# Banded attention values: two row quarters in one product of 64 rows and 48 columns

## The chip, the cores and the metric

The kernel runs on one core of a Trainium2 chip. The metric is device microseconds from start to end of one execution. Engines are named as the profile names them: PE is TensorE's matrix product, PEld its weight load, DVE is VectorE, ACT is ScalarE, POOL is GpSimd, SP is SyncE, which issues the DMAs here.

## What is computed

An attention of two scales, over 4 batches, 8 heads, 576 positions and head size 64, is followed by two gated feed-forward layers over its 2304 tokens. Only the attention's banded half is touched here; cut to it, the reference is:

```python
pos = np.arange(S)                                    # S = 576
mask = np.abs(pos[:, None] - pos[None, :]) < 4
scores = np.where(mask, q @ k.T / 8, -1e9)            # per batch and head
attn = np.exp(scores - scores.max(-1))
attn = attn / (attn.sum(-1) + 1e-9)
out_local = attn @ v                                  # the banded values
return out_up + out_local                             # out_up: attention over means of 4 positions
```

## The kernel before

**Jobs.** A job is one batch and one pair of heads, 16 in all, called (b, hp) below. A query meets only the keys at most 3 positions away, so the 576 queries are cut into 24 tiles of 24 queries (`NQ`), each with its 30 keys (`NU`). Four tiles stand at a time in the four quarters of 32 partitions; `NG` = 6 such groups and the two heads h make the 24 x 2 tiles of a job.

**Steps of a job.** PE makes the band scores (line 813) and the pooled scores (line 866) in one PSUM buffer `pa` of two banks. DVE subtracts the maxima (849, 850), ACT takes the exponential into `pt` (853), DVE sums, inverts and multiplies by the inverse (854, 856, 857) and transposes each block of 32 x 32 (858) from `pt` into `tt`, so that keys lie on partitions. Then `band` (960 to 969) multiplies: for group g, quarter i and head h one product has the 30 value rows of that quarter as weights (64 columns, `vt`) and the quarter's 24 probability columns as the moving side. Half of the quarters (0 and 2, then 1 and 3) go in one call, 24 products a call, two calls a job. In all jobs but (0,0) and (1,0), which the code marks as not `merged`, the first call stands in front of the transposes of the pooled probabilities (`down_t`, 951) and the second in front of the pooled values (`values`, 989). ACT copies the transposes out (957); `combine` on DVE adds both halves (1002).

**What sets the order.** The code first records every operation with engine, planned duration, due time and buffers; `Plan.order` then simulates the engines with those planned durations and writes a fixed order for each of the five queues. `ATT` is the time that the plan sets aside for a batch's attention in a feed-forward visit. So a job's small products stand between the large products of a feed-forward visit: the attention of batches 1 to 3 is spread over the feed-forward work of batches 0 to 2, from about 44 to 365 us. PE also waits for the weights of the large products: each block of 128 x 512 weights is split by ACT (`whi`, line 1055) and by DVE or POOL (`wlo`, its low part, 1058), in a ring of four buffers, and is used by twelve products (1119 to 1121). On PE every float32 product of the band is recorded as two pieces, so 24 products appear as x48.

Of the kernel before, what the change touches and what calls it, by code (L numbers as in the profile page):

```python
# [10 lines left out]
F32 = mybir.dt.float32  # L11
# [5 lines left out]
AF = mybir.ActivationFunctionType  # L17
# [350 lines left out]
def tile_multiscale_attention_gated_ffn(  # L368
# [95 lines left out]
    for nm, n, shape in (("qt", 2, [P, S + 8]), ("kt", 2, [P, KPAD + S + 5]), ("vt", 0, [P, NG, VC]),  # L464
                         ("sc", 1, [P, 2, NG, NU]), ("pt", 2, [P, 2, NG, 32]), ("tt", 2, [P, 2, NG, 32]),
                         ("vg", 1, [GH, 2, 4, VC]), ("half", 1, [P, G, 2]),
                         ("qd", 2, [P, G]), ("kd", 2, [P, G]), ("vd", 2, [GH, 2, VC]),
                         ("pd", 2, [GH, 2, 2, G]), ("pdt", 1, [GH, 2, 2, G]), ("up", 2, [P, G]), ("ones", 1, [P, 102]),
                         ("xf", 2, [P, S])):
        aslots += ring(nm, n, shape, F32, apool)  # L470

# [159 lines left out]
    QUANTUM = 3 * 227.0  # L631
    ATT = 15.0e3
    T0 = 30.0e3
# [106 lines left out]
    class Job:  # L740
# [48 lines left out]
        def pools(self):  # L789
            for nm in ("qd", "kd", "sc", "nm", "sm", "pd", "nmd", "smd", "pt", "tt"):  # L790
                setattr(self, nm, self.buf(nm))
# [5 lines left out]
        def scores(self):  # L797

            ss = bank(self.banks)
            qt, kt, sc, pt, tt, nm, sm = self.qt, self.kt, self.sc, self.pt, self.tt, self.nm, self.sm  # L800
            n = NG * NU
# [32 lines left out]
            if not masked:  # L834
                op("dve", dve_ns(2 * n), lambda: nc.vector.tensor_add(
                    sc.t.rearrange("p h g c -> p h (g c)"), ss.t[:, :, :n],
                    maskb[:, None, :].to_broadcast([P, 2, n])), [ss], [sc], when)
            if self.merged:
# [7 lines left out]
            def scores_of():  # L846
                return ss.t[:, :, :n].rearrange("p h (g c) -> p h g c", c=NU) if masked else sc.t

            op("dve", dve_ns(2 * n), lambda: nc.vector.reduce_max(nm.t, scores_of(), axis=AX.X), [x], [nm], at)
            op("dve", dve_ns(2 * n), lambda: nc.vector.tensor_sub(sc.t, scores_of(), spread(nm)),  # L850
               [nm, x] if masked else [nm], [sc], at, port=not masked)
            p = pt.t[:, :, :, :NU]
            op("act", act_ns(2 * n), lambda: nc.scalar.activation(p, sc.t, AF.Exp, scale=SCALE), [sc], [pt], at)
            op("dve", dve_ns(2 * n), lambda: nc.vector.reduce_sum(sm.t, pt.t[:, :, :, :NU + 1], axis=AX.X),
# [4 lines left out]
                out=tt.t.rearrange("p h g c -> p (h g c)"), in_=pt.t.rearrange("p h g c -> p (h g c)")),  # L859
               [pt], [tt], at)  # L860

        def pooled(self, ss, c):
# [73 lines left out]
        def down_t(self):  # L936
# [23 lines left out]
        def band(self, x, ss):  # L960

            vt, tt, v0 = halves[self.b, self.hp // 2].vt, self.tt, self.hp % 2 * P
            for g in range(NG):
                for s, i in ((0, x), (1, 2 + x)):
                    ks, q = slice(32 * i, 32 * i + NU), NQ * (NG * x + g)
                    for h in range(2):
                        nc.tensor.matmul(ss.t[h * D:(h + 1) * D, s, q:q + NQ],  # L967
                                         vt.t[ks, g, v0 + h * D:v0 + (h + 1) * D], tt.t[ks, h, g, :NQ],
                                         start=True, stop=True, tile_position=(32 * i, h * D))

        def values(self):

            b, hp = self.b, self.hp
            early = self.merged
            ss = self.ss if early else bank(self.banks)
            half = halves[b, hp // 2]
            vd, vt, pdt, tt = half.vd, half.vt, self.pdt, self.tt
            up = buf("up")  # L980
# [4 lines left out]
            def pe():  # L985
                self.band(int(early), ss)
                for kh in range(2):
# [10 lines left out]
            if not early:  # L998
                op("pe", 700.0, lambda: self.band(1, ss), [vt, tt, up], [ss], at, heat=90.0, words=96)
# [568 lines left out]


    op("act", act_ns(P), lambda: nc.scalar.copy(identb.t, ident.t), [ident], [identb], 0.0)  # L1570
    jobs = [Job(b, hp) for b in range(B) for hp in range(NHP)]
# [7 lines left out]
    for n in range(len(jobs) + 1):  # L1579
# [80 lines left out]
```

## Time and profile before

| what | us |
|---|---|
| time, median of 3 runs | 911.86 (911.67 to 912.22) |
| the profiled execution's own time | 911.72 |
| its span, first to last instruction | 909.7 |
| PE busy | 899.0 (99%) |
| DVE busy | 700.4 (77%) |
| ACT busy | 530.5 (58%) |
| POOL busy | 70.1 (8%) |

The span is the part of the execution that the instructions cover; 2.0 us lie around it. PE's records overlap, because matmuls are pipelined: the time that a stretch costs on PE is read from start to start in the timeline, not from the durations. The granted clock is 0.999 of full speed over the span.

### The profile page before, as it was taken

The page shows a single profiled execution, that of the slowest core. Times are in us where ns is not written, and L with a number is a line of the kernel's source. Part 1 is how long each engine was busy: PE and PEld are TensorE (multiplying, and loading weights), DVE is VectorE, ACT ScalarE, POOL GpSimd, SP SyncE. Part 2 cuts the span into 40 slices and gives each one's busy share as a digit, 9 for nine tenths or more (in the row PEclk, how much of TensorE's full clock was granted, in tenths as well). Part 3 has the DMA queues.
Part 4 walks back from the last instruction along what each step waited for, and adds up shares of the span by engine and source line. Part 5 has one row for each costly group of instructions (what it writes and reads, how often), then busy time and mean ns, then how long its engine had stood idle before and what let it go on. Part 6 is the DMA issues. An engine that isn't in the chain of part 4 may idle for free.

```text
span 909.7 us, 18862 instructions
## 1 busy us (share of the span) xinstructions
PE 899.0 (99%) x7369; PEld 758.6 (83%) x7369; DVE 700.4 (77%) x1322; ACT 530.5 (58%) x1119; POOL 70.1 (8%) x103
## 2 busy tenths in 40 slices
PE   7999999999999999999999999999999999999998
PEld 5787878878888877899999998888888988888886
DVE  8987885676567666899999898778976779877642
ACT  4687874666656666755554655444665655535541
POOL 4011110111011100010000000000301001000000
PEclk9999999999999999999999999999999999999999
DMA  8769581664466635343212651103531002000531
GB/s 254 235 207 257 177 206 48 197 164 167 156 189 197 210 110 183 97 156 117 96 41 65 218 182 46 47 24 106 175 117 66 1 1 70 36 36 35 174 93 47
DMA packets 65675, 113.75 MB, mean 125 GB/s; under 512 B 8433, under 2 KB 29755, under 8 KB 65586
## 3 DMA queue, kind: packets, MB, share of 16 engines
q1 hardware_dynamic: 65586, 112.54, 40.0%
q8 instruction: 58, 0.95, 0.5%
q14 instruction: 31, 0.25, 0.1%
HBM read 82.37 MB, written 30.15 MB: 124 GB/s over the span
## 4 chain that ended last, share of the span: by engine, by line
PE 98%; DVE 1%; POOL 0%; issue 0%; ACT 0%; POOLq 0%
PE ph L1119 14%; PE ph L1120 13%; PE ph L1121 13%; PE acc L1119 9%; PE acc L1121 9%; PE acc L1120 9%; PE pa L1119 7%; PE pa L1120 7%; PE pa L1121 7%; PE pa L967 2%; PE pa L813 1%; PE pa L866 1%; PE pa L989 1%; PE pa L951 1%; PE acc L1611 1%; PE acc L724 1%
## 5 line engine op out<-in xcount | busy, mean ns | idle before, releaser
L1119 PE MATMUL ph<-xhi,whi 128*128 128x512 f32 (+1 forms) x344 | 134.6, 391 | 0.0
L1120 PE MATMUL ph<-xhi,wlo 128*128 128x512 f32 (+1 forms) x344 | 131.6, 382 | 0.0
L1121 PE MATMUL ph<-xlo,whi 128*128 128x512 f32 (+1 forms) x344 | 131.5, 382 | 0.0
L1055 ACT CAST whi<-w 128x512 fp32r<-128x512 f32 x140 | 85.4, 611 | 57.5 <-PE ph L1121 30.0
L1058 DVE TENSOR_TENSOR wlo<-w,whi 128x512 fp32r<-128x512 f32 x137 | 94.3, 690 | 27.7 <-ACT whi L1055 27.3
L1058 DVE TENSOR_TENSOR wlo<-wr,whi 128x512 fp32r<-128x512 f32 x106 | 68.5, 648 | 36.8 <-ACT whi L1055 35.2
L1119 PEld LDWEIGHTS ph<-xhi,whi 128*128 128x128 f32 x344 | 64.7, 188 | 15.4 <-issue 2.0
L1121 PEld LDWEIGHTS ph<-xlo,whi 128*128 128x128 f32 x344 | 64.7, 188 | 12.9
L1055 ACT CAST whi<-wr 128x512 fp32r<-128x512 f32 x106 | 60.2, 570 | 26.1 <-PE acc L1121 12.9
L1120 PEld LDWEIGHTS ph<-xhi,wlo 128*128 128x128 f32 x344 | 64.7, 188 | 11.7
L1119 PE MATMUL acc<-ghi,whi 128*128 128x512 f32 (+1 forms) x192 | 73.5, 383 | 0.0
L1121 PE MATMUL acc<-glo,whi 128*128 128x512 f32 (+1 forms) x192 | 72.3, 376 | 0.4 <-DVE glo L1058 0.4
L1120 PE MATMUL acc<-ghi,wlo 128*128 128x512 f32 (+1 forms) x192 | 72.2, 376 | 0.0
L1235 DVE TENSOR_TENSOR w<-pa,w 128x512 f32<-128x512 f32 (+1 forms) x112 | 70.2, 627 | 2.6 <-PE pa L1121 2.1
L1055 ACT CAST w<-w 128x512 fp32r<-128x512 f32 x62 | 37.9, 619 | 43.2 <-PE acc L1120 22.0
L1119 PE MATMUL pa<-w,whi 128*128 128x512 f32 (+1 forms) x166 | 60.7, 366 | 0.1
L1121 PE MATMUL pa<-w,whi 128*128 128x512 f32 (+1 forms) x166 | 60.7, 365 | 0.0
L1120 PE MATMUL pa<-w,wlo 128*128 128x512 f32 (+1 forms) x166 | 60.6, 365 | 0.0
L1058 DVE TENSOR_TENSOR w<-w,w 128x512 fp32r<-128x512 f32 x58 | 41.2, 715 | 18.8 <-ACT w L1055 18.8
L1160 DVE SCALAR_TENSOR_TENSOR th<-th,ph 128x512 f32<-128x512 f32 (+1 forms) x44 | 28.0, 637 | 27.6 <-PE ph L1121 23.0
L1155 ACT ACTIVATE th<-ph 128x512 f32<-128x512 f32 (+1 forms) x44 | 24.6, 559 | 39.6 <-PE ph L1121 39.4
L1119 PEld LDWEIGHTS acc<-ghi,whi 128*128 128x128 f32 x192 | 36.0, 188 | 7.4 <-issue 1.7
(311 smaller groups left out, 2204.4 us busy)
## 6 DMA issues: line engine op xcount, KB each, us to landing
w<-w SPq DMA_DIRECT2D x56, 512.0 KB
w2d<-we SPq DMA_DIRECT2D x32, 256.0 KB
w<-gd SPq DMA_DIRECT2D x32, 256.0 KB
gd<-w SPq DMA_DIRECT2D x30, 256.0 KB
st<-x2d SPq DMA_DIRECT2D x52, 128.0 KB
w<-w SPq DMA_DIRECT2D x24, 256.0 KB
w<-w2d SPq DMA_DIRECT2D x16, 256.0 KB
wr<-w2d SPq DMA_DIRECT2D x16, 256.0 KB
```

The costliest lines, as they stand in the source:

```text
L724: nc.tensor.matmul(ss.t[:GH, kh, :VC], ones.t[ks, o:o + GH], vt.t[ks, g], start=g == 0, stop=g == NG - 1, tile_position=(64 * kh, 0))
L813: nc.tensor.matmul(ss.t[32 * i:32 * i + 32, h, g * NU:(g + 1) * NU], qt.t[hs, NQ * t:NQ * t + 32], kt.t[hs, NQ * t:NQ * t + NU], start=not ...
L866: nc.tensor.matmul(ss.t[:GH, h, c + r * G:c + (r + 1) * G], qd.t[h * D:(h + 1) * D, r * GH:(r + 1) * GH], kd.t[h * D:(h + 1) * D, :], star ...
L967: nc.tensor.matmul(ss.t[h * D:(h + 1) * D, s, q:q + NQ], vt.t[ks, g, v0 + h * D:v0 + (h + 1) * D], tt.t[ks, h, g, :NQ], start=True, stop=T ...
L1055: op("act", act_ns(n), lambda: nc.scalar.copy(vh(), vm()), [rm], [rh], due)
L1058: return lambda: on.tensor_sub(vl(), vm(), vh().bitcast(F32))
L1119: nc.tensor.matmul(o, lhi, rhi, start=first, stop=False, skip_group_check=more)
L1120: nc.tensor.matmul(o, llo, rhi, start=False, stop=False, skip_group_check=more)
L1121: nc.tensor.matmul(o, lhi, rlo, start=False, stop=last, skip_group_check=more)
L1155: op("act", act_ns(n, True), lambda h=h: nc.scalar.activation(th.t[:, :n], h.t[:, :n], AF.Tanh, scale=0.5 if layer == 1 else 1.702 / 4.0), ...
L1160: op("dve", dve_ns(n), lambda: nc.vector.scalar_tensor_tensor(th.t[:, :n], th.t[:, :n], 1.0, hb[-1].t[:, :n], op0=ALU.add, op1=ALU.mult), ...
L1235: op("dve", dve_ns(N), lambda: nc.vector.tensor_add(tmp.t[:, o, :N], b.t[:, :N], tmp.t[:, i, :N]), [b, (tmp, i)], [(tmp, o)], t)
```

## The change

For batches 1 to 3 the two calls of `band` become one call of `bands`, which takes two neighbouring quarters (64 rows) in one product: the probabilities of the two quarters stand as a block diagonal, s = 0 and s = 1, so that 64 value rows meet 2 x 24 = 48 columns, and the zeros in the block keep the quarters apart. A job has 24 products of 64 rows x 48 columns in place of 48 products of 30 rows x 24 columns. The call stands in `values`; `down_t` keeps only its transposes. Batch 0 stays as it was.

The block diagonal is made by DVE. `parity` holds 1 or 0 by quarter and s; the inverse sums are multiplied by it into 24 columns (`smw`), and one product of 720 elements writes the exponentials times `smw` to `ptw`, so that a quarter's other half becomes zero. The exponential now stays in `sc`, which has one more column for the 1e-9. The transpose is over 768 elements. `ptw` and `ttw` lie over the two former buffers of `pt` and `tt`, so there is one of each, not two.

The diff, cut to its core:

```diff
-                         ("sc", 1, [P, 2, NG, NU]), ("pt", 2, [P, 2, NG, 32]), ("tt", 2, [P, 2, NG, 32]),
+                         ("sc", 1, [P, 2, NG, NU + 1]), ("pt", 0, [P, 2, NG, 32]), ("tt", 0, [P, 2, NG, 32]),
...
+            both = apool.tile([P, 2, *shape[1:]], F32, name=nm, tag=nm)
+            plan.ring(nm, [Slot(both[:, i]) for i in range(2)])
+            plan.ring(nm + "w", [Slot(both.rearrange("p n h g c -> p (n h g c)").rearrange(
+                "p (h g s c) -> p h g s c", h=2, g=NG, s=2), tuple(plan.rings[nm][0]))])
...
+    nc.vector.memset(plan.rings["sc"][0][0].t[:, :, :, NU:NU + 1], 1.0e-9)
...
-    ATT = 15.0e3
+    ATT = 13.0e3
...
+        def wide(self, at, n):
...
+            op("act", act_ns(n), lambda: nc.scalar.activation(p, p, AF.Exp, scale=SCALE), [], [sc], at)
+            op("dve", dve_ns(n), lambda: nc.vector.reduce_sum(sm.t, sc.t[:, :, :, :NU + 1], axis=AX.X),
+               [sc], [sm], at)
+            op("dve", 155.0, lambda: nc.vector.reciprocal(sm.t, sm.t), [], [sm], at)
+            op("dve", 155.0, lambda: nc.vector.tensor_mul(
+                smw.t, sm.t.rearrange("p h g -> p (h g)")[:, :, None].to_broadcast([P, 2 * NG, 2]),
+                parity.t[:, None, :].to_broadcast([P, 2 * NG, 2])), [sm, parity], [smw], at, port=True)
+            op("dve", dve_ns(2 * n), lambda: nc.vector.tensor_mul(
+                ptw.t.rearrange("p h g s c -> p (h g) s c")[:, :, :, :NU],
+                hg(sc.t)[:, :, None, :NU].to_broadcast([P, 2 * NG, 2, NU]),
+                smw.t[:, :, :, None].to_broadcast([P, 2 * NG, 2, NU])), [sc, smw], [ptw], at, port=True)
+            op("dve", dve_ns(NG * 128), lambda: nc.vector.transpose(
+                out=ttw.t.rearrange("p h g s c -> p (h g s c)"), in_=ptw.t.rearrange("p h g s c -> p (h g s c)")),
+               [ptw], [ttw], at)
...
             if self.merged:
-                c, due, more = HALF // 2, 0.5, [halves[self.b, self.hp // 2].vt, self.tt]
+                due = 0.5
+            if self.merged and not self.b:
+                c, more = HALF // 2, [halves[self.b, self.hp // 2].vt, self.tt]
...
-                if self.merged:
+                if more:
                     self.band(0, ss)
...
+        def bands(self, ss):
+            vt, ttw, v0 = halves[self.b, self.hp // 2].vt, self.ttw, self.hp % 2 * P
+            for g in range(NG):
+                for i in range(2):
+                    ks, q = slice(64 * i, 64 * i + 64), NQ * g
+                    for h in range(2):
+                        o = ss.t[h * D:(h + 1) * D, i, :HALF].rearrange("p (s q) -> p s q", s=2)
+                        nc.tensor.matmul(o[:, :, q:q + NQ], vt.t[ks, g, v0 + h * D:v0 + (h + 1) * D],
+                                         ttw.t[ks, h, g, :, :NQ], start=True, stop=True, tile_position=(64 * i, h * D))
...
-                self.band(int(early), ss)
+                if wide:
+                    self.bands(ss)
+                else:
+                    self.band(int(early), ss)
...
-            op("pe", 1400.0, pe, [vd, pdt, vt, tt], [ss, up, xf], at, heat=300.0, words=112)
+            op("pe", 1500.0 if wide else 1400.0, pe, [vd, pdt, vt, tt], [ss, up, xf], at, heat=300.0, words=112)
...
-            if x < len(front):
-                front[x]()
-            if x < len(back):
-                back[x]()
+            for some in (front, back) if n <= NHP else (back, front):
+                if x < len(some):
+                    some[x]()
```

The written order moves too. In the two pieces below the large products of a feed-forward visit are 1119 to 1121 before and 1176 to 1178 now; 967 was `band` and 1021 is `bands`; 951 and 993 are the pooled transposes, 989 and 1046 the pooled values.

PE's queue at the last job, (3,3), before:

```order
L1121 MATMUL ph_149<-xlo_91,whi_81 128x512
L967 MATMUL pa_159<-tt_129,vt 64x24 x24
L951 MATMUL pa_159<-ident,pd_139 72x72 x8
L1119 MATMUL ph_149<-xhi_89,whi_81 128x512
...
L1121 MATMUL ph_150<-xlo_91,whi_78 128x512
L967 MATMUL pa_159<-tt_129,vt 64x24 x24
L989 MATMUL pa_159<-pdt_140,vd_137 64x144 x4
```

and now:

```order
L1178 MATMUL ph_147<-xlo_91,whi_81 128x512
L993 MATMUL pa_157<-ident,pd_137 72x72 x8
L1176 MATMUL ph_147<-xhi_89,whi_81 128x512
...
L1178 MATMUL ph_148<-xlo_91,whi_78 128x512
L1021 MATMUL pa_157<-tt,vt 64x2x24 x24
L1046 MATMUL pa_157<-pdt_138,vd_135 64x144 x4
```

The first of the job's two band calls is gone from the queue; the one that is left has the second's place, twelve large products behind the transposes, as before.

DVE's queue at job (2,1), from the sum of the exponentials to the first low parts of weights behind the transpose, before:

```order
L854 TENSOR_REDUCE small<-pt_127 128x12
L856 RECIPROCAL small<-small 128x12
L1164 TENSOR_TENSOR glo_96<-th_98,ghi_94 128x512
L857 TENSOR_TENSOR pt_127<-pt_127,small 128x12x30
L858 STREAM_TRANSPOSE tt_129<-pt_127 128x384
L1058 TENSOR_TENSOR wlo_83<-w_112,whi_79 128x512
L1058 TENSOR_TENSOR wlo_84<-wr_108,whi_80 128x512
```

and now, where 1115 makes the low parts (1058 before) and 1221 is the former 1164:

```order
L888 TENSOR_REDUCE small<-sc_125 128x12
L1221 TENSOR_TENSOR glo_96<-th_98,ghi_94 128x512
L890 RECIPROCAL small<-small 128x12
L894 TENSOR_TENSOR pt<-sc_125,ones_141 128x24x30
...
L1115 TENSOR_TENSOR wlo_83<-w_112,whi_79 128x512
L898 STREAM_TRANSPOSE tt<-pt 128x768
L1115 TENSOR_TENSOR wlo_84<-wr_108,whi_80 128x512
```

The product and the transpose are twice as wide, and one low part now stands between them.

## Rows read from the trace of the kernel before

**Rows 1.** The page: busy us of each engine, share of the span, instructions.

```profile
PE 899.0 (99%) x7369; PEld 758.6 (83%) x7369; DVE 700.4 (77%) x1322; ACT 530.5 (58%) x1119; POOL 70.1 (8%) x103
```

**Rows 2.** Waits of PE, all: engine, line, releaser, us, times, longest us.

```profile
PE pa L807 <- ACT identb L1570: 4.9, 1, 4.9
...
PE acc L1121 <- DVE glo L1058: 0.4, 1, 0.4
```

**Rows 3.** Busy time by stretch: stretch, length, PE, PEld, DVE, ACT, POOL busy (count).

```profile
60.00:143.00 83.00, 83.00 (x1051) 66.64 (x1050) 65.30 (x112) 62.00 (x135) 8.71 (x12) 1.00 0.69 194
...
sum 303.00, PE 303.00 PEld 244.22 DVE 211.76 ACT 199.88 POOL 28.12; mean PE 101.00 PEld 81.41 DVE 70.59 ACT 66.63 POOL 9.37
```

**Rows 4.** PE's timeline at job (1,1): start us, us, engine, line, shapes, count.

```profile
84.42 0.39 PE L1121 MATMUL acc<-glo,whi 128*128 128x512 f32 x1
84.73 0.89 PE L967 MATMUL pa<-tt,vt 30*64 30x24 f32 x48
85.56 0.69 PE L951 MATMUL pa<-ident,pd 72*72 72x72 f32 x8
...
86.37 0.39 PE L1120 MATMUL acc<-ghi,wlo 128*128 128x512 f32 x1
```

**Rows 5.** PE's timeline at job (1,0), whose transposes stand without a band call.

```profile
63.03 0.39 PE L1119 MATMUL acc<-ghi,whi 128*128 128x512 f32 x1
...
63.48 0.39 PE L1121 MATMUL acc<-glo,whi 128*128 128x512 f32 x1
63.71 0.66 PE L951 MATMUL pa<-ident,pd 72*72 72x72 f32 x8
...
64.49 0.40 PE L1120 MATMUL ph<-xhi,wlo 128*128 128x512 f32 x1
```

**Rows 6.** PE's timeline around the second, separate band call of job (1,0).

```profile
77.25 0.39 PE L1121 MATMUL ph<-xlo,whi 128*128 128x512 f32 x1
...
78.73 0.40 PE L1120 MATMUL ph<-xhi,wlo 128*128 128x512 f32 x1
```

**Rows 7.** Lines 967, 813, 866: ns min/median/max, first and last start us.

```profile
L967 PEld LDWEIGHTS pa<-tt,vt x1248: 127/133/134, 28.5 to 363.0; 30*64 30x64 f32 x179
L967 PE MATMUL pa<-tt,vt x1248: 210/211/233, 28.5 to 363.0; 30*64 30x24 f32 x179
...
L813 PEld LDWEIGHTS pa<-kt,qt x1248: 102/106/154, 5.3 to 346.2; 64*32 64x32 f32 x179
L813 PE MATMUL pa<-kt,qt x1248: 184/191/258, 5.3 to 346.2; 64*32 64x30 f32 x179
...
L866 PE MATMUL pa<-kd,qd x112: 282/283/341, 12.4 to 346.7; 64*72 64x144 f32 x112
```

**Rows 8.** Timeline of products and weight loads near 76 us.

```profile
75.98 0.50 PE L1119 MATMUL ph<-xhi,whi 128*128 128x512 f32 x1
76.09 0.19 PEld L1120 LDWEIGHTS ph<-xhi,wlo 128*128 128x128 f32 x1
```

**Rows 9.** Groups on DVE by line and shape: count, busy us, mean ns, idle before.

```profile
L1002 DVE TENSOR_TENSOR xf<-pa,up 128x576 f32<-128x576 f32 x13 | 9.8, 755 | 4.6 <-ACT up L996 3.3 <-PE pa L967 1.3
L858 DVE STREAM_TRANSPOSE tt<-pt 128x384 f32<-128x384 f32 x14 | 8.0, 575 | 0.3
L857 DVE TENSOR_TENSOR pt<-pt,small 128x360 f32<-128x360 f32 x14 | 7.6, 543 | 0.2
```

**Rows 10.** Timeline: band values of job (1,0), transpose of job (1,1).

```profile
74.52 0.89 PE L967 MATMUL pa<-tt,vt 30*64 30x24 f32 x48
...
75.09 0.58 DVE L858 STREAM_TRANSPOSE tt<-pt 128x384 f32<-128x384 f32 x1
```

**Rows 11.** Timeline: low parts behind job (2,1)'s transpose, and the products that follow.

```profile
199.24 1.45 DVE L1058 TENSOR_TENSOR wlo<-wr,whi 128x512 fp32r<-128x512 f32 x2
...
201.24 0.39 PE L1119 MATMUL acc<-ghi,whi 128*128 128x512 f32 x1
```

**Rows 12.** Busy time behind the attention, columns as in rows 3.

```profile
380.00:460.00 80.00, 79.91 (x439) 76.90 (x438) 76.91 (x174) 45.33 (x101) 4.74 (x6) 1.00 0.38 117
```

More of the change, by code (lines that the diff above doesn't have):

```diff
@@ L469, in tile_multiscale_attention_gated_ffn @@
                          ("xf", 2, [P, S])):
-        aslots += ring(nm, n, shape, F32, apool)
+        if n:
+            aslots += ring(nm, n, shape, F32, apool)
+        elif nm != "vt":
+            both = apool.tile([P, 2, *shape[1:]], F32, name=nm, tag=nm)
+            plan.ring(nm, [Slot(both[:, i]) for i in range(2)])
+            plan.ring(nm + "w", [Slot(both.rearrange("p n h g c -> p (n h g c)").rearrange(
+                "p (h g s c) -> p h g s c", h=2, g=NG, s=2), tuple(plan.rings[nm][0]))])
+            aslots += [*plan.rings[nm][0], *plan.rings[nm + "w"][0]]
+    one = plan.rings["ones"][0][0]
+    plan.ring("smw", [Slot(one.t[:, :4 * NG].rearrange("p (x s) -> p x s", s=2), (one,))])
+    plan.ring("parity", [Slot(one.t[:, 4 * NG:4 * NG + 2], (one,))])
+    aslots += [*plan.rings["smw"][0], *plan.rings["parity"][0]]
     def parts_in(x, *sizes):
@@ L789, in pools @@
         def pools(self):
-            for nm in ("qd", "kd", "sc", "nm", "sm", "pd", "nmd", "smd", "pt", "tt"):
+            for nm in ("qd", "kd", "sc", "nm", "sm", "pd", "nmd", "smd", *(("ptw", "smw") if self.b else ("pt", "tt"))):
                 setattr(self, nm, self.buf(nm))
@@ L799, in scores @@
             ss = bank(self.banks)
-            qt, kt, sc, pt, tt, nm, sm = self.qt, self.kt, self.sc, self.pt, self.tt, self.nm, self.sm
+            qt, kt, sc, nm, sm = self.qt, self.kt, self.sc, self.nm, self.sm
             n = NG * NU
@@ L835, in scores @@
                 op("dve", dve_ns(2 * n), lambda: nc.vector.tensor_add(
-                    sc.t.rearrange("p h g c -> p h (g c)"), ss.t[:, :, :n],
-                    maskb[:, None, :].to_broadcast([P, 2, n])), [ss], [sc], when)
+                    sc.t[:, :, :, :NU], ss.t[:, :, :n].rearrange("p h (g c) -> p h g c", c=NU),
+                    mask[:, None].to_broadcast([P, 2, NG, NU])), [ss], [sc], when)
             if self.merged:
@@ L846, in scores_of @@
             def scores_of():
-                return ss.t[:, :, :n].rearrange("p h (g c) -> p h g c", c=NU) if masked else sc.t
+                return ss.t[:, :, :n].rearrange("p h (g c) -> p h g c", c=NU) if masked else sc.t[:, :, :, :NU]
             op("dve", dve_ns(2 * n), lambda: nc.vector.reduce_max(nm.t, scores_of(), axis=AX.X), [x], [nm], at)
-            op("dve", dve_ns(2 * n), lambda: nc.vector.tensor_sub(sc.t, scores_of(), spread(nm)),
+            op("dve", dve_ns(2 * n), lambda: nc.vector.tensor_sub(sc.t[:, :, :, :NU], scores_of(), spread(nm)),
                [nm, x] if masked else [nm], [sc], at, port=not masked)
+            if self.b:
+                return self.wide(at, 2 * n)
+            pt, tt = self.pt, self.tt
             p = pt.t[:, :, :, :NU]
-            op("act", act_ns(2 * n), lambda: nc.scalar.activation(p, sc.t, AF.Exp, scale=SCALE), [sc], [pt], at)
+            op("act", act_ns(2 * n), lambda: nc.scalar.activation(p, sc.t[:, :, :, :NU], AF.Exp, scale=SCALE), [sc], [pt], at)
             op("dve", dve_ns(2 * n), lambda: nc.vector.reduce_sum(sm.t, pt.t[:, :, :, :NU + 1], axis=AX.X),
@@ L860, in scores @@
                [pt], [tt], at)
+        def wide(self, at, n):
+            self.ttw = buf("ttw")
+            sc, sm, smw, ptw, ttw = self.sc, self.sm, self.smw, self.ptw, self.ttw
+            if (self.b, self.hp) == (1, 0):
+                op("dve", 120.0, lambda: nc.vector.memset(
+                    ptw.t.rearrange("p h g s c -> p (h g s) c")[:, :, NU:NU + 1], 0.0), [], [ptw], at)
+            p = sc.t[:, :, :, :NU]
+            hg = lambda x: x.rearrange("p h g c -> p (h g) c")
+            op("act", act_ns(n), lambda: nc.scalar.activation(p, p, AF.Exp, scale=SCALE), [], [sc], at)
[12 more added lines that the diff above has]
+               [ptw], [ttw], at)
         def pooled(self, ss, c):
@@ L976, in values @@
             early = self.merged
+            wide = b > 0
             ss = self.ss if early else bank(self.banks)
             half = halves[b, hp // 2]
-            vd, vt, pdt, tt = half.vd, half.vt, self.pdt, self.tt
+            vd, vt, pdt, tt = half.vd, half.vt, self.pdt, self.ttw if wide else self.tt
             up = buf("up")
@@ L994, in values @@
             at = self.due(0.6 if early else 0.9)
-            op("pe", 1400.0, pe, [vd, pdt, vt, tt], [ss, up, xf], at, heat=300.0, words=112)
+            op("pe", 1500.0 if wide else 1400.0, pe, [vd, pdt, vt, tt], [ss, up, xf], at, heat=300.0, words=112)
             op("act", 285.0, lambda: nc.scalar.activation(up.t, ss.t[:, 0, c0:c0 + G], AF.Copy, scale=0.25),
                [ss], [up], at)
-            if not early:
+            if not early and not wide:
                 op("pe", 700.0, lambda: self.band(1, ss), [vt, tt, up], [ss], at, heat=90.0, words=96)
@@ L1567, in tile_multiscale_attention_gated_ffn, with make_parity @@
     op("dve", 700.0, make_ones, [ident], [ones], -20.0e3)
+    parity = buf("parity")
+    def make_parity():
+        for i in range(4):
+            for n in range(2):
+                nc.vector.memset(parity.t[32 * i:32 * i + 32, n:n + 1], float(i % 2 == n))
+    op("dve", 560.0, make_parity, [], [parity], T0 + 20.0e3, T0 + 20.0e3)
     op("act", act_ns(P), lambda: nc.scalar.copy(identb.t, ident.t), [ident], [identb], 0.0)
```

## Prediction

> **What bounds the kernel now.** The page comes first: PE is busy 99% of the span [rows 1]. As its records overlap, that alone proves little, so the waits of PE come next: three in the whole run, 4.9 + 1.2 + 0.4 us, the two long ones ahead of 20 us [rows 2]. So between 20 us and the end nothing that PE waits for is worth naming, and what a stretch costs is what PE's queue holds there. Next come the busy times of the stretch where the changed jobs lie, 60 to 363 us: PE 303.00 of 303 us, DVE 211.76, ACT 199.88, at a granted clock of 1.00 [rows 3]. DVE has 91 us to spare there, and is densest in the first stretch, 65.30 of 83. A microsecond taken from PE's queue there is a microsecond off the end, as long as the other engines keep their lead. What each piece of the queue costs is read from start to start in PE's timeline [rows 4 to 6].
>
> **What goes from PE.** Eleven of the twelve changed jobs have a band call ahead of the transposes. There, from the start of the last large product in front to the start of the second one behind, it takes 86.37 - 84.42 = 1.95 us [rows 4]; at (1,0), where the transposes stand alone, 64.49 - 63.48 = 1.01 us [rows 5]. So a call there costs 0.94 us, its entry and exit included, and eleven cost 10.3. At (1,0) the second call stands alone: 78.73 - 77.25 = 1.48 us [rows 6], of which two large products would take 63.48 - 63.03 = 0.45 [rows 5]; it costs 1.03. Together 11.37 us go.
>
> **What the call that is left costs.** It is 24 products, 48 recorded pieces, as before, but with 64 rows and 48 columns in place of 30 and 24. No row shows that form, so it is bounded. The four products of a group lie on four parts of the array and run side by side in rounds, two rounds of pieces to a group, 12 to a call. A call lasts 85.56 - 84.73 = 0.83 us with its drain, so a round is at most 69 ns [rows 4]. What fills a round? A piece with 144 moving columns is recorded with 283 ns, one with 30 columns with 191: 92 ns for 114 columns, 0.81 ns a column [rows 7]. By that the band's piece with 24 columns should show 186; it shows 211, so 25 ns of it are spent waiting. Its weight load is recorded with 133 ns for 64 columns, against 106 for the 32 columns of line 813, 0.84 ns a column [rows 7]: 64 columns take some 54 ns and 24 moving columns 19. A round is thus the 54 ns of its weights, with the moving side hidden beneath. 48 columns take 39 ns, still under 54, and the weights stay 64 columns wide. I take the call's time as unchanged, except that the last round cannot hide its moving side: 24 more columns, 0.02 us, twelve times 0.24 us.
>
> The upper end: loads and products on the same rows take turns, and every round grows by the 19 ns of the new columns: 12 rounds x 12 jobs x 19 ns = 2.7 us. The lower end: the load of 54 ns is peculiar to the 30-row form, and a round falls to the 39 ns of its columns and the same 4 ns or so of spacing that lie beyond the 54: 12 x 12 x 11 ns, less the overhang kept above, 1.5 us of gain. I take the middle, since the recorded load is read at 64 columns, which the change keeps.
>
> The Trainium skill, in "TensorE: Matmul & The Clock Gate", Part 3 on packing small matmuls, states that a weight load overlaps products in flight only when its row group differs; the new calls have only two row groups, both always in use, so by it the upper end holds. Here the trace speaks against that rule: a load over all 128 rows starts at 76.09 us under a product over the same rows that started at 75.98 and is recorded for 0.50 us [rows 8]. It is kept below as a rival.
>
> **What DVE gets, and what hides it.** From 360 elements (543 ns) to 576 (755 ns) a DVE operation grows by 0.98 ns an element over a fixed 0.19 us [rows 9]. The product of 720 elements should take 0.90 us against 0.54, the small one of 24 elements 0.21, the transpose of 768 elements 0.97 by the same slope against 0.575, or 1.15 if it only scales. That is 0.96 us more a job, 1.14 at most, 11.5 us over twelve jobs, inside the 91 us of idle time [rows 3]. Two low parts of weights go from DVE to POOL. None of this is on PE's path unless something PE needs comes late. Two things could. First, the transposed probabilities: at (3,3) the surviving call stands twelve large products behind the pooled transposes, where the second call stood, and the first, which needed them earlier, is gone; so these have 2.7 us and more of extra lead for the extra 0.96. Second, the low parts queued behind the transpose. The tightest place I find, by counting low parts against groups of products from the start of the run, is behind (2,1)'s transpose: the first of two parts starting at 199.24 us is done near 199.9, and products start at 201.24 on the part made before it, a lead of 1.9 us, while most others have 4 to 10 [rows 11]. The extra 0.96 fits, and the new order puts one low part between the wide product and the transpose there. If that cover were gone, PE would pay 0.96 us a job, 11.5 in all.
>
> The single `ttw` adds a wait. On PE the scores of a job stand behind the band values of the one before, except at (1,1), whose transpose starts at 75.09 us while the values of (1,0) are being multiplied from 74.52 to about 75.35 [rows 10]. There DVE's transpose, with the next low part and `combine` behind it, waits 0.3 us or so for PE; the leads above cover it. ACT's exponential only changes where it writes. The extra memset at the start (0.07 us by its size, an estimate from the 0.1 to 0.2 us that the fixed part of any small operation costs) comes ahead of DVE work on which PE waited 1.2 us [rows 2], so I count 0.1 us. The eight small memsets of `parity` lie in DVE's idle time. The shorter `ATT` moves due times, no work.
>
> **The sum.** 11.37 - 0.24 - 0.1 = 11.0 us. The profiled execution took 911.72 us, its span 909.7; 911.72 - 11.0 = 900.7. The median of the three runs is 0.14 above the profiled one, so 900.8 against it; I name **900.8 us**.
>
> **Rivals.**
> - *Weights and columns take turns* (upper end): 900.8 + 2.7 = 903.5 us. For it: no row shows a part of 64 rows and 64 columns at work. Against it: [rows 7, 8]. Chance 0.11.
> - *The load is shorter with 64 rows* (lower end): 900.8 - 1.5 = 899.3. It is within the range, not given a chance of its own.
> - *DVE takes some back behind the attention.* From 380 to 460 us DVE is busy 76.91 of 80 us [rows 12]. If it enters that stretch later relative to PE, because the last batch's jobs gave it 4 x 0.96 us more and took 4 x 0.94 from PE, PE waits for the sum of what cannot be caught up; if the whole gain of that batch goes, 3.8 us, 904.6. Against it: before 363 DVE has a third of its time idle [rows 3]. Chance 0.07.
> - *The change doesn't do what it says*: a call's time goes by columns after all, so that 24 products of 48 columns cost what 48 of 24 did. Then only the entries and exits go: of the 0.94 some 0.26 (0.94 less the 0.68 of twelve rounds at 57 ns), 12 x 0.26 = 3.1 us, 908.8. Against it: [rows 7]. Chance 0.03.
> - *Slower: the wide DVE chain makes the low parts late in every job.* With leads of 2 to 4 us behind the transposes, PE loses nothing until the chain has grown by that much; to eat 0.92 us of gain a job it must grow by about 4 us, not 0.96. That takes a product of 720 elements with two repeated operands running at 5 ns an element and more. If the chain grew by 5 us, PE would lose some 2 us a job, 24 us: 925. Against it: line 857 already repeats one operand and takes 543 ns, as other operations of its size. Chance 0.04. A wait of like size that just eats the gain, for no change: 0.03.
>
> **How the numbers follow.** Forecast 0.72, taking turns 0.11, given back 0.07, by columns 0.03, no change 0.03, slower 0.04. All but the last two are faster by over 0.2% (1.8 us, about what a measurement of this kernel can tell from no change): faster 0.93, same 0.03, slower 0.04. The range runs from the lower end, 899.2, to the given-back case, 904.7; beyond it lie 0.10, and a little for missed sizes.
>
> **What would show it.** In the profile after: the products of `bands` x48 with about 0.85 us from their start to that of the pooled values behind (1.07 if they take turns, 0.7 at the lower end); the transposes with 1.01 us from the product in front to the second behind, as in [rows 5]; no wait of PE over 0.5 us between 20 and 450 us; the wide DVE product near 0.90 us and the transpose near 0.97. The prediction is wrong if PE shows waits on low parts or on the wide transpose, or if the call is longer than 1.1 us.

## The result, and the profile after

The changed kernel takes **900.96 us**, median of four runs (900.33 to 901.83), against 911.85 us before: a ratio of 0.9881 with an interval of 0.9864 to 0.9898, 10.9 us faster. The forecast was 900.8. The profiled execution is the slowest of the four, 901.83 us with a span of 900.0; its own saving is 911.72 - 901.83 = 9.9 us, and the difference between 9.9 and the 11.0 of the sum has to be found too.

PE is still the engine that sets the end. First the page's line of busy times, then all waits of PE (engine, line, releaser, us, times, longest us) of the changed kernel:

```profile
PE 888.5 (99%) x6793; PEld 750.1 (83%) x6793; DVE 710.3 (79%) x1341; ACT 529.0 (59%) x1119; POOL 74.3 (8%) x106
```

```profile
PE pa L819 <- ACT identb L1635: 4.9, 1, 4.9
PE pa L825 <- issue: 0.6, 1, 0.6
PE ph L1178 <- DVE glo L1115: 0.6, 1, 0.6
PE acc L993 <- DVE pd L963: 0.5, 1, 0.5
PE acc L1177 <- issue: 0.5, 1, 0.5
PE acc L1178 <- DVE glo L1115: 0.5, 1, 0.5
```

Against [rows 1], PE's busy time fell by 10.5 us (the sum says 11.0) and DVE's rose by 9.9 (the prediction's 11.5, less some 1.3 us of two low parts of weights that POOL now makes). Against [rows 2], two waits are new behind 20 us: "issue" ahead of a product of line 1177 (a wait for nothing that the profile shows, at 296.3 us) and one on a low part of activations, line 1115, at 506 us.

The busy times of the stretches that answer to [rows 3] (60 to 363 us) and [rows 12]; columns are the stretch, its length, and busy us and count of PE, PEld, DVE, ACT, POOL, then PE's granted clock, the busy share of the DMA engines and GB/s:

```profile
60.00:363.00 303.00, 302.49 (x3039) 244.34 (x3038) 225.95 (x378) 203.46 (x455) 32.45 (x43) 1.00 0.58 179
380.00:460.00 80.00, 79.91 (x453) 78.67 (x452) 77.57 (x170) 44.30 (x94) 5.00 (x7) 1.00 0.34 107
```

DVE rose by 14.2 us in 303, with the work of a somewhat longer part of the program in it, and kept 77 us idle.

PE's timeline at the transposes of job (1,1) and at the values of job (1,0): start us, us, line, operation, tiles, shapes, count.

```profile
83.45 0.39 PE L1178 MATMUL acc<-glo,whi 128*128 128x512 f32 x1
83.68 0.66 PE L993 MATMUL pa<-ident,pd 72*72 72x72 f32 x8
84.14 0.48 PE L1176 MATMUL acc<-ghi,whi 128*128 128x512 f32 x1
84.46 0.40 PE L1177 MATMUL acc<-ghi,wlo 128*128 128x512 f32 x1
```

```profile
74.24 0.39 PE L1178 MATMUL acc<-glo,whi 128*128 128x512 f32 x1
74.56 0.92 PE L1021 MATMUL pa<-tt,vt 64*64 64x48 f32 x48
75.41 0.71 PE L1046 MATMUL pa<-pdt,vd 72*64 72x144 f32 x8
76.05 0.50 PE L1176 MATMUL ph<-xhi,whi 128*128 128x512 f32 x1
76.38 0.39 PE L1177 MATMUL ph<-xhi,wlo 128*128 128x512 f32 x1
```

The transposes stand alone: 84.46 - 83.45 = 1.01 us, where [rows 4] had 1.95. The new call lasts 75.41 - 74.56 = 0.85 us to the pooled values behind it; in [rows 4] the old one lasted 0.83 to the transposes. From the large product in front to the second one behind, the whole block of values takes 76.38 - 74.24 = 2.14 us, against 76.32 - 74.20 = 2.12 us in the kernel before; to the nanosecond the traces have 2.139 to 2.140 us in the twelve jobs, against 2.119 to 2.120. The same block of job (1,0) before:

```profile
74.20 0.39 PE L1121 MATMUL acc<-glo,whi 128*128 128x512 f32 x1
...
75.34 0.71 PE L989 MATMUL pa<-pdt,vd 72*64 72x144 f32 x8
...
76.32 0.40 PE L1120 MATMUL ph<-xhi,wlo 128*128 128x512 f32 x1
```

DVE's new operations, with ns min/median/max and the first and last start, and count by shape:

```profile
L894 DVE TENSOR_TENSOR pt<-sc,ones x12: 908/909/1064, 50.9 to 342.1; 128x720 f32<-128x720 f32 x12
...
L898 DVE STREAM_TRANSPOSE tt<-pt x12: 971/972/980, 53.5 to 343.1; 128x768 f32<-128x768 f32 x12
...
L891 DVE TENSOR_TENSOR ones<-small,ones x12: 169/182/185, 50.7 to 341.9; 128x24 f32<-128x24 f32 x12
```

Where the 9.7 us of the span come from, counted along the large products of the two traces (the k-th of one against the k-th of the other):

| piece | forecast | measured |
|---|---|---|
| eleven transposes lose the call ahead of them | +10.3 | 11 x 0.941 = +10.35 |
| the lone second call of (1,0) | +1.03 | +1.025 |
| twelve calls of the new form | -0.24 | 12 x 0.020 = -0.24 |
| the start | -0.1 | +0.14 |
| gaps in two score calls (67.2 and 233.9 us) | not named | -0.40 |
| "issue" gap at 296.3 us | not named | -0.68 |
| wait on a low part at 506 us | not named | -0.75 |
| after the last product | not named | +0.3 |
| sum | 11.0 | 9.7 |

Every piece that the prediction priced came out within 0.05 us, but for the start, which was 0.2 better. What it did not price took 1.5 us in this execution. The quickest of the four is 11.5 us below the median before; it has no trace, so what it lost is not shown.

### The profile page after: what moved, and what is told of

Its sections match the earlier page's. It is cut to its first block, busy times and chain, and to the rows that moved or that the text cites. A ratio compares the mean times of both kernels' runs of the same rounds, so it can differ in the third digit from the quotient of the medians.

```text
span 900.0 us, 17750 instructions
## 1 busy us (share of the span) xinstructions
PE 888.5 (99%) x6793; PEld 750.1 (83%) x6793; DVE 710.3 (79%) x1341; ACT 529.0 (59%) x1119; POOL 74.3 (8%) x106
## 4 chain that ended last, share of the span: by engine, by line
PE 98%; DVE 2%; issue 0%; ACT 0%; DVEq 0%
PE ph L1176 14%; PE ph L1178 14%; PE ph L1177 14%; PE acc L1176 9%; PE acc L1178 9%; PE acc L1177 9%; PE pa L1176 8%; PE pa L1178 8%; PE pa L1177 8%; PE pa L825 1%; PE pa L1021 1%; PE pa L906 1%; PE pa L1046 1%; PE pa L993 1%; PE acc L1675 1%; PE acc L736 1%
## 5 line engine op out<-in xcount | busy, mean ns | idle before, releaser
L1115 DVE TENSOR_TENSOR wlo<-wr,whi 128x512 fp32r<-128x512 f32 (+1 forms) x105 | 67.6, 644 | 31.8 <-ACT whi L1112 30.7
```

What stands on the lines that cost most here:

```text
L1115: return lambda: on.tensor_sub(vl(), vm(), vh().bitcast(F32))
```

## Experiments

Three questions were put: what fills a round of the new call, whether PE's queue alone sets the end and how far DVE's work is covered, and what the gaps and the order have to do with it. Beside each run stands its median; the changed kernel as a control had 901.32 us. The kernel before, on the same chips, had 911.74 (control, halves, less VectorE work), 911.76 (more VectorE work, spacing of 15) and 911.96 us (the call twice, spacings of 12 and 13).

**The control.** The changed kernel again, no edit.

> The changed kernel once more, unaltered. In its first profile the blocks of PE saved what the prediction's steps say (eleven transposes 0.94 us each, the lone call 1.03, twelve calls 0.02 longer: 11.1 us), but the span fell by 9.7 only. Missing: 0.2 us in the middle of two score calls (67.2 and 233.9 us), 0.7 at 296.3, 0.9 in two waits on low parts of activations at 497 and 506. Theory: these are a matter of the single execution or of DMA traffic, so some of them are gone or elsewhere here, the blocks measure the same to 0.01 us, and the median is 900.3 to 901.8. Rival: the waits at 497 and 506 belong to the changed order and come again in the same size; then a profiled execution saves 9.4 to 10.3 us again.

Measured: 901.32 us (900.82 to 901.86), ratio 0.9885 (0.9870 to 0.9899). The blocks were the same to 0.01 us. Its waits of PE behind 60 us:

```profile
PE acc L1177 <- issue: 0.8, 1, 0.8
PE acc L1178 <- DVE glo L1115: 0.4, 1, 0.4
```

The gap at 296 us came again, with 0.92 us over the usual spacing; the wait at 506 was gone, and the one at 497 stands in the kernel before as well [rows 2]. The two score calls were longer again, 2.04 for 1.85 us and 1.81 for 1.59. So the theory held for 506 alone. There the trace shows the chain: DVE's `ev` waited for the DMA that had last stored from its buffer, and the low part of activations stood behind it. DVE's timeline of the first profile, then of the control:

```profile
505.04 0.56 DVE L1369 TENSOR_SCALAR ev<-acc 128x384 f32<-128x384 f32 x1 [1.54 <-DMA x2d<-ev]
505.51 0.55 DVE L1115 TENSOR_TENSOR glo<-w,ghi 128x384 fp32r<-128x384 f32 x1
```

```profile
504.76 0.56 DVE L1369 TENSOR_SCALAR ev<-acc 128x384 f32<-128x384 f32 x1 [0.61 <-DMA x2d<-ev]
505.24 0.55 DVE L1115 TENSOR_TENSOR glo<-w,ghi 128x384 fp32r<-128x384 f32 x1
```

The bracket is the idle time ahead of the instruction and what ended it: 1.54 us in the one, 0.61 in the other.

**What fills a round: half the weight columns.**

```
- o = ss.t[h * D:(h + 1) * D, i, :HALF].rearrange(...)
+ o = ss.t[h * D:h * D + 32, i, :HALF].rearrange(...)
- ... vt.t[ks, g, v0 + h * D:v0 + (h + 1) * D], ...
+ ... vt.t[ks, g, v0 + h * D:v0 + h * D + 32], ...
```

> Half the weights: each product of bands loads 32 of its 64 columns (32 of the 64 value columns of a head are left out). Theory: a round is the 54 ns of the load of 64 columns with the moving side beneath it; with 32 columns the load takes 27 ns, and the 39 ns of the 48 moving columns and some 4 to 7 of spacing take its place: a call is 12 x 8 to 11 ns shorter, 0.10 to 0.13 us, twelve calls 1.2 to 1.6 us. Loads and columns taking turns: 12 x 27 ns, 0.32 us a call, 3.9 us. A round set by columns or by the issue of pieces: no change.

**Half the moving columns.**

```
- nc.tensor.matmul(o[:, :, q:q + NQ], ..., ttw.t[ks, h, g, :, :NQ], ...)
+ nc.tensor.matmul(o[:, 0, q:q + NQ], ..., ttw.t[ks, h, g, 0, :NQ], ...)
```

> Half the moving columns: each product of bands multiplies 24 of its 48 columns (one of two row quarters is left out). Theory: rounds stay at their load, only the last round's columns stand out: a call is 0.02 us shorter (block of values 1.466 for 1.486 us), twelve 0.24 us, no change that can be measured. Loads and columns taking turns: 12 x 19 ns, 0.23 us a call, 2.7 us in all. A round set by columns alone: as much.

Measured: half the weights 898.08 us (897.82 to 898.99), half the moving columns 901.08 (900.55 to 901.18). The values of job (1,0) on PE's timeline, first with half the weights, then with half the columns:

```profile
75.05 0.71 PE L1021 MATMUL pa<-tt,vt 64*32 64x48 f32 x48
75.70 0.71 PE L1046 MATMUL pa<-pdt,vd 72*64 72x144 f32 x8
76.34 0.50 PE L1176 MATMUL ph<-xhi,whi 128*128 128x512 f32 x1
```

```profile
75.50 0.90 PE L1021 MATMUL pa<-tt,vt 64*64 64x24 f32 x48
76.32 0.71 PE L1046 MATMUL pa<-pdt,vd 72*64 72x144 f32 x8
76.96 0.50 PE L1176 MATMUL ph<-xhi,whi 128*128 128x512 f32 x1
```

With 24 columns the call is 0.82 us, 0.02 to 0.03 shorter than with 48, and the block of values 2.119 us for 2.139: the 0.020 us of the forecast. So the columns are hidden, and the case in which loads and columns take turns (2.7 us) is out. With 32 weight columns the call is 0.65 us and the block 1.942, 0.197 us less, twelve times 2.4 us. From the raw starts a round of four pieces takes 59 ns in the kernel before, in the changed kernel and with half the columns, and 42 to 43 ns with half the weights. That the load is what fills the round is shown. Both times fit a round that is the longer of two sides that overlap, the weights' 54 ns or the columns' 39 as the prediction estimates them from [rows 7], and some 4 more. That the columns are what ends the shorter round is only argued: with 32 weight columns and 24 moving ones this would give a still shorter round, a load with a larger fixed part would not, and no run has that form. The expectation had 8 to 11 ns a round and 1.2 to 1.6 us; it took the 54 ns for the whole round and left out the 4 on the one side. Of the 3.2 us between the medians 2.4 are in the blocks. The two profiled executions differ by 2.6 us of span (897.2 against the control's 899.8); where the rest lies is not shown.

The Trainium skill, "TensorE: Matmul & The Clock Gate", Part 3, lets a weight load overlap products in flight only where the row group differs. Both row groups of this call are busy all the time, and 24 more columns a piece cost 0.02 us a call and not 12 x 0.019 = 0.23; nor has a round of 59 ns room for 54 of load and 39 of columns in turn. Part 2 of the same page of the Trainium skill has a wider condition, a row group without conflict or a background buffer for the weights; with that these runs agree.

**Is PE's queue the end?** The call made twice in a row.

```
- self.bands(ss)
+ self.bands(ss) or self.bands(ss)
```

> The bands call made twice in a row in each of the twelve jobs, with the same result; no other engine gets work, and the order is the same. It prices a call where it stands. Theory: PE's queue sets the end, so a second call costs its twelve rounds of 59 ns on the end, 0.70 us each (no second entry and exit): 12 x 0.70 = 8.5 us, 909.6 against 901.1 to 901.3. Rival: some of the call lies under waits of PE that would be there anyway: then less than 8 us. If the second call has to drain the first: 0.85 us each, 10.2 us, 911.4.

Measured: 910.82 us (909.0 to 911.45). The blocks are 2.839 for 2.139 us in all twelve jobs, 0.70 each, 8.4 together, as the rounds say. The time grew by 9.5 against the control, 1.1 more. The trace shows one gap that is larger than the control's of 0.9 us at 296 us, again "issue", in the ninth score call, 1.7 us over the usual spacing:

```profile
300.32 0.72 PE L825 MATMUL pa<-kt,qt 64*32 64x30 f32 x60
302.57 0.49 PE L825 MATMUL pa<-kt,qt 64*32 64x30 f32 x36 [1.53 <-issue]
```

The microseconds of PE's queue do come off and go on at the end one for one; the gaps go on top.

**Is DVE's work covered?** First less of it: product and transpose at half their elements in batches 2 and 3.

```
- self.ttw = buf("ttw")
+ m, self.ttw = 1 if self.b > 1 else 2, buf("ttw")
...
- ptw.t...[:, :, :, :NU], hg(sc.t)[:, :, None, :NU].to_broadcast([P, 2 * NG, 2, NU]), smw.t[:, :, :, None]...
+ ptw.t...[:, :, :m, :NU], hg(sc.t)[:, :, None, :NU].to_broadcast([P, 2 * NG, m, NU]), smw.t[:, :, :m, None]...
...
- out=ttw.t.rearrange(...), in_=ptw.t.rearrange(...)
+ out=ttw.t.rearrange(...)[:, :384 * m], in_=ptw.t.rearrange(...)[:, :384 * m]
```

> The wide product and the wide transpose at their old sizes in batches 2 and 3 (half the elements are left out, old values stay there): 8 jobs with some 0.37 + 0.40 us less on VectorE, 6.2 us, with PE's queue unaltered. Theory: the extra work of VectorE is hidden, so the span up to 363 us is the same to 0.1 us, and the time is 900.3 to 901.8. Rival: part of the gain is given back behind the attention because VectorE comes there later; then the waits at 497 and 506 us shrink or go and up to 0.9 us is gained.

Measured: 901.18 us (900.46 to 901.81), the control's time. The two operations fell to 0.53 and 0.58 us in eight jobs, DVE's busy time in 60 to 363 us from the first profile's 225.95 to 220.10, and PE's blocks did not move. The gap at 296 us and the wait at 506 are missing in this profile; as the control lacks the wait at 506 too, nothing speaks for the rival.

Then more of it: the wide product three times, and five times.

```
- op("dve", dve_ns(2 * n), lambda: nc.vector.tensor_mul(ptw.t..., ..., smw.t...),
+ op("dve", dve_ns(2 * n), lambda: [nc.vector.tensor_mul(ptw.t..., ..., smw.t...) for _ in range(3)],
```

> The wide product made three times in each of the twelve jobs: 2 x 0.91 = 1.82 us more on VectorE a job, same order on every engine, same result. Theory: the leads of low parts behind the transposes (1.9 us the smallest found before, of which the change took 0.96; most others 4 to 10) and of the transposed probabilities cover nearly all: at most some 1 us at the tightest job, 901 to 902. Rival: VectorE is already at its limit in these stages, and each added microsecond comes out on PE: up to 12 x 1.82 = 22 us, 923.

> The wide product made five times: 4 x 0.91 = 3.64 us more on VectorE a job, 43.7 us over twelve. VectorE has 303.0 - 226.0 = 77 us idle from 60 to 363 us. Theory: the leads of 2 to 4 us are used up in some jobs; PE waits on low parts of weights or on the wide transpose in several, 905 to 925. If the leads are longer than read, 901 to 903; if VectorE is at its limit, 944.

Measured: three times 901.66 us (901.04 to 902.45), ratio 0.9878 (0.9860 to 0.9896), no more than the control can tell; five times 914.84 us (913.35 to 915.7), slower than the kernel before by 1.0025 (1.0014 to 1.0035). The cover holds for 1.8 us more a job and is gone with 3.6. The waits of PE with the product made five times:

```profile
PE acc L1177 <- DVE wlo L1115: 2.8, 3, 1.2
PE acc L1176 <- DVE ev L1369: 2.7, 1, 2.7
PE acc L993 <- DVE pd L963: 1.2, 1, 1.2
PE ph L1177 <- DVE wlo L1115: 1.1, 2, 0.9
PE ph L1176 <- DVE th L1217: 0.6, 1, 0.6
```

The wait on `pd` lies ahead of 20 us, as in the kernel before. The others are what the prediction named, low parts queued behind the chain, and beside them two it did not name: the copy `ev` that frees an accumulator, and `th`. One of the places, in DVE's and PE's timeline:

```profile
289.98 3.77 DVE L894 TENSOR_TENSOR pt<-sc,ones 128x720 f32<-128x720 f32 x3
...
293.79 0.98 DVE L898 STREAM_TRANSPOSE tt<-pt 128x768 f32<-128x768 f32 x1
294.69 0.65 DVE L1115 TENSOR_TENSOR wlo<-wr,whi 128x512 fp32r<-128x512 f32 x1
295.26 0.68 DVE L1369 TENSOR_SCALAR ev<-acc 128x512 f32<-128x512 f32 x1
...
295.99 0.50 PE L1176 MATMUL acc<-ghi,whi 128*128 128x512 f32 x1 [2.67 <-DVE ev L1369]
```

The products, the transpose and a low part stand ahead of `ev`, and PE waits 2.7 us for it. Summed over all places this run lost 13.4 us up to 363 us, and its span is 13.2 longer than in the first profile. Some 3 us of that are no wait but a lower granted clock, told in the last section.

Last, extra DVE work on the kernel before, with PE's queue as it was: the transpose three times in batches 1 to 3.

```
- op("dve", 500.0, lambda: nc.vector.transpose(...),
+ op("dve", 500.0, lambda: [nc.vector.transpose(...) for _ in range(3 if self.b else 1)],
```

> The kernel before, with the transpose of the probabilities made three times in batches 1 to 3: 2 x 0.575 = 1.15 us more on VectorE a job, somewhat more than the change adds (0.96), everything else as before. It prices the change's VectorE work without its PE side. Theory: hidden, 911.7 to 912.5. Rival: up to 12 x 1.15 = 13.8 us, 925.6.

Measured: 912.06 us (911.57 to 915.43), ratio 1.0002 (0.9990 to 1.0014). DVE's share of the change costs nothing that can be measured, on either kernel.

**The order.** The spacing of due times alone, on the changed kernel at 15 and 12, and on the kernel before at 13.

```
- ATT = 13.0e3
+ ATT = 15.0e3
```

> The changed kernel with the attention's spacing of due times back at the old 15 us for 13 (order alone; no operation is added or removed). Theory: the saving is what left PE's queue, so the time stays within 0.3% of 901; the waits on low parts may stand elsewhere. Rival: the shorter spacing is itself a part of the gain: then up to some us slower, with PE waits between 60 and 460 us.

> The changed kernel with the spacing of due times at 12 for 13 us (order alone). If the waits that are left (0.6 to 0.9 us at 296 us, 0.6 us at 497 and some at 506) hang on the order, they move or go, and 900 to 900.5 can come out; if the order around 380 us is again one in which PE waits, 902 to 904. By the theory nothing else changes, since PE's operations are the same.

> The kernel before with the shorter spacing of due times (13 for 15 us) alone: the order part of the change without its products. The changed kernel with 15 took 902.9 us and showed PE waits of 2.1 us at 381.9 to 384.0 us, which it lacks with 13. Theory A: the spacing only makes up for what the shorter PE queue does to the order behind the attention, so alone on the kernel before it brings nothing: 911.2 to 912.5. Theory B: it is a gain of its own: 910 to 910.5. Theory C: it makes the kernel before worse, by waits of PE: over 912.5.

Measured: the changed kernel at 15 902.90 us (902.14 to 903.7), at 12 901.55 (900.68 to 902.27); the kernel before at 13 911.47 (911.04 to 913.99), ratio 0.9997 (0.9988 to 1.0005). At 15 a wait behind the attention shows in PE's timeline:

```profile
383.55 0.51 PE L1176 MATMUL acc<-ghi,whi 128*128 128x512 f32 x1 [1.28 <-ACT ghi L1220]
384.02 0.49 PE L1177 MATMUL acc<-ghi,wlo 128*128 128x512 f32 x1
384.62 0.50 PE L1178 MATMUL acc<-glo,whi 128*128 128x512 f32 x1
```

Three products in a row come late, 2.3 us against the control there; the gap at 296 us is missing in that profile (0.9 us back), and between the medians 1.6 us are left. So the spacing is no gain of its own, and 12 is no better than 13; at 15 the changed kernel loses time behind the attention, the place that the rival "DVE takes some back" had named, with ACT's high part `ghi` as the last to come; that DVE is the reason is not shown. The order of the two loops (`back` ahead of `front`) was not tried alone.

**The gaps.** Two band calls of batch 0 made twice, so that all behind them stands 96 records later in PE's program.

```
- self.band(int(early), ss)
+ [self.band(int(early), ss) for _ in range(2 if self.hp in (1, 2) else 1)]
```

> The changed kernel with two band calls of batch 0 (jobs 1 and 2) made twice, ahead of 40 us, with the same result: all that follows on PE stands 96 records later in its program. Asked is what the gaps inside PE's calls hang on, which no wait on another engine explains: 0.2 us inside the score calls at 66.4 and 232.9 us (PE records 1253 and 2918 to 2920 from the start) and 0.7 to 0.9 us at 296 us (record 3531). Theory: they belong to the count of PE's instructions from the start (instructions arrive in blocks). Then the score calls at 66.4 and 232.9 us are back at their undisturbed 1.85 and 1.59 us; record 2920 is now in the bands call of job (2,2) near 227 us, whose block shows about 1.7 us for 1.486; and record 3531 is in the score call near 294 us, which shows 0.2 us and more on top of its 1.59. Rival: they belong to what runs there (these score calls, these transfers): then the same two calls are longer by 0.2 us again and no bands call is.

Measured, in a single execution of 902.76 us: the same two score calls are longer again, 2.04 and 1.84 us, now at records 1345 and 3024, the bands call of (2,2) has its 1.486 us, and the gap at 296 us is gone. The seventh score call, first of the changed kernel, then of this run, with the eighth of the changed kernel as an undisturbed one ahead of them:

```profile
272.57 1.02 PE L825 MATMUL pa<-kt,qt 64*32 64x30 f32 x96
```

```profile
232.89 1.23 PE L825 MATMUL pa<-kt,qt 64*32 64x30 f32 x96
```

```profile
235.47 1.26 PE L825 MATMUL pa<-kt,qt 64*32 64x30 f32 x96
```

So for the 0.2 us inside the score calls the theory fell: they don't hang on the count of PE's records from the start. They come again in the same two calls in the first profile, the control, both halves, with less VectorE work and here; with a spacing of 15 or 12 neither call has them, and with the call made twice the seventh has none. What PE waits for there stays open.

For the gap at 296 us this run decides less than it seems, and the other traces decide more. Each trace also holds the packets of a queue of instructions, q8 on the page of the changed kernel (packets, MB, share):

```profile
q8 instruction: 53, 0.87, 0.4%
```

It follows PE's program: 53 packets of 16 KB for 13586 weight loads and products, and 58 for 14738 in the kernel before, so some 256 instructions a packet. In the 14 traces, those of the kernel before and its two variants among them, PE has twelve waits behind 20 us that the profile puts down to "issue". The product held up is always the 477th, 605th, 733rd, 989th, 3533rd or 3917th of PE's records. With the semaphore waits counted in, a whole number of 256 instructions lies between any two of these places: they are edges between two packets. And each of the twelve waits ends 1.3 to 1.6 us after the last q8 packet ahead of it has landed; at no edge behind 20 us, in any of the traces, does the first product start sooner than 1.1 us after that. The line of the gap in the first profile, then the product at this edge in seven runs (us):

```profile
297.04 0.39 PE L1177 MATMUL acc<-ghi,wlo 128*128 128x512 f32 x1 [0.51 <-issue]
```

| run | packet landed | product in front starts | product starts | over the usual spacing |
|---|---|---|---|---|
| the changed kernel | 295.58 | 296.13 | 297.04 | 0.68 |
| the control | 296.38 | 296.65 | 297.80 | 0.92 |
| half the weights | 294.14 | 294.62 | 295.57 | 0.72 |
| half the moving columns | 295.56 | 296.73 | 297.07 | 0.10 |
| the call twice (3917th) | 301.13 | 300.85 | 302.57 | 1.72 |
| less VectorE work | 294.50 | 296.25 | 296.48 | 0 |
| spacing of 15 | 292.10 | 296.67 | 296.90 | 0 |

The later the packet lands against the product's turn, the longer the gap, and with 1.7 us or more to spare there is none. So PE waits there for its own instructions, a packet of which lands late. In the run with 96 products more in front the 3533rd product lies inside the ninth score call, and its packet had landed 15 us ahead: no gap, and nothing against the count. That run has its gap at another edge, 1.0 us at 40.40 us. Why a packet starts late (at 294.34 us in the changed kernel, at 291.13 with a spacing of 15) stays open.

The Trainium skill, "Runtime: NRT & Kernel Launch", section "Instruction fetch mechanics", states that an engine's instructions are refilled in blocks of 256 while it runs, and that crossing a block is mostly hidden. The traces agree on both: 256 instructions a packet, and of the 50 or so edges of a run at most two show such a wait behind 20 us.

## Why the prediction was right, step by step

- *PE's queue is the end.* Right. The call made twice costs 0.70 us a job in the blocks and no less at the end; work taken from DVE or given to it moves nothing until its cover is gone.
- *What goes.* Right: 0.941 us eleven times, 1.025 once.
- *What the new call costs.* Right, 0.020 us a job, and for the reason given: the load of 64 columns fills a round, and only the last round shows its columns. The *lower end* was mis-sized in its working: it compared the columns' 39 ns and 4 of spacing with a load of 54 without spacing, 11 ns a round; halving the load shows 16 to 17, as if the spacing were in both. The end would have been 2.4 us of gain in place of 1.5, a little below the range's 899.2.
- *DVE.* Right on the durations (0.909 for 0.90, 0.972 for 0.97, 0.182 for 0.21 us) and on the cover; but the slope that it names, 0.98 ns an element, gives 0.95 us for the transpose, so that the 0.97 came out so exactly is luck. The single `ttw` was to make (1,1)'s transpose wait 0.3 us: its group shows no idle time ahead of it, as the low part now stands in front of it and fills that stretch. The leads were read too simply as counts of low parts: with more DVE work `ev` and `th` are as late as the low parts. The slower rival's point holds: with a chain 0.96 + 3.64 = 4.6 us longer than before the gain is gone, 914.8 us, where the prediction had 925 for a growth of 5; but some 3 us of that loss are a lower granted clock, which it did not name.
- *"The shorter ATT moves due times, no work."* True, and too little. With the old spacing the changed kernel waits behind the attention, and 1.6 us of the gain go. The rival of 0.07 had named the place, not the size (3.8 us) nor the engine: the last to come there is ACT's `ghi`. With the spacing that the change brings, the wait is not there.
- *No wait of PE over 0.5 us between 20 and 450 us.* Wrong by one, the gap of 0.7 to 0.9 us at 296 us: PE's own instructions are a term that the sum does not have. This, the two score calls (0.4) and the wait at 506 in one of the two profiles are 1.8 and 1.3 us that the sum lacks. The start and the end gave back 0.4. So the profiled execution, 901.83 us, came 1.1 later than the 900.7 of the sum; that the median is within 0.2 us of the forecast is in part luck, since how much of these gaps the quicker executions have is not shown.

## What to carry to other kernels

Where one engine is busy all the time, price a change by the spacing of that engine's own queue, from the last undisturbed instruction in front to the first behind, with and without the piece; eleven blocks read so were right to a few nanoseconds. When small products are packed, look which of two overlapping sides, weight columns or moving columns, fills a round: the other was doubled here for 0.02 us a call. And an idle share of an engine (25% here) says little on how much a single job's chain may grow; that is told by the distance to the next thing that someone waits for, and it ended between 1.8 and 3.6 us a job. Where the busy engine stops and no other engine is the reason, look whether its own instructions had landed: waits of 0.2 to 1.5 us stood at the edges of their packets here.

## What the runs showed that was not expected

A few late products cost more than their wait. With the wide product made five times, PE waited near 109 to 111 us and again near 293 to 296, and behind each the granted clock was at the lower of its two levels (1.2 of 2.4 GHz) for some 3.4 us, as the means of 0.83 over 10 us and 0.84 over 11 say. Stretch, length, PE, PEld, DVE, ACT, POOL busy, the granted clock as a mean, the busy share of the DMA engines and GB/s:

```profile
107.00:117.00 10.00, 8.52 (x37) 6.07 (x36) 9.44 (x15) 7.74 (x15) 0.00 (x0) 0.83 0.34 106
290.00:301.00 11.00, 8.32 (x35) 6.44 (x34) 9.10 (x11) 4.67 (x8) 4.77 (x5) 0.84 0.78 193
```

Large products stand 427 ns apart there, for 227 elsewhere, which costs some 1.6 us each time, about 3 of the run's 13.4 us. In the changed kernel the clock is 1.00 in both stretches.
